# The second product of a mixture of experts in seven products for eight, on transposed sums

## The chip, the cores and the metric

The kernel runs on one core of a Trainium2 chip. Its metric is the time of one execution on the device in microseconds (us), as the median of several runs; the profile is that of one execution more.

## The reference

Three stages follow one another. An attention with 4 batches of 8 heads, 576 positions and head width 64 (a block-causal mask, softmax) gives x with 2304 tokens of 512 values. Then a mixture of 8 experts:

```python
def _moe_ref(x, w_gate, w1, w2):          # N, D, E, F = 2304, 512, 8, 1024
    logits = x @ w_gate
    P = np.exp(logits - logits.max())
    for _ in range(8):                    # rows, then columns, brought to their sums
        P /= P.sum(1, keepdims=True) + 1e-09
        P /= P.sum(0, keepdims=True) + 1e-09
        P *= N / E
    out = np.zeros((N, D), dtype=np.float32)
    for e in range(E):
        h = np.maximum(x @ w1[e], 0.0)
        out += P[:, e:e + 1] * (h @ w2[e])
    return out
```

Last comes a two-layer block with w_in (512 x 1024), a softmax-weighted activation, a normalisation and w_out (1024 x 512). Everything is float32, and a plain float32 product isn't what the kernel uses: it splits each operand into a high part that TensorE's fp32r format holds and a low rest, and makes three products of them (high x low, low x high, high x high).

## The kernel before, in words

All 2304 tokens are computed on one core. Attention comes first, and while it runs the first expert (expert 0) is filled in between, segment by segment of finished tokens: `moe` (L507) makes the hidden values of 128 columns of w1 at a time and then, tile by tile of 128 tokens, the second product, which it adds up in `accs` (L71, 18 tiles of 128 tokens x 512). `sinkhorn` (L390) brings the gate weights `pr` to their sums.

Experts 1 to 7 follow in three passes of 768 tokens (`work`, L810). A unit is half an expert's 1024 hidden columns, so there are 14 units in a pass and 42 in all. In a unit, `first_layer` (L642) computes a block of hidden values, transposed (hidden columns on the partitions, tokens along), with seven block products where eight would be plain: the 512 input values and the 768 tokens are cut into two halves each, and the unit's 512 hidden columns into two halves of two groups of 128 columns. The left factors (sums and differences of w1's blocks, numbered 1 to 7) are made and split by `left_factors` (L584) in pass 0, kept in DRAM (`fdram`, L86) and loaded again in passes 1 and 2; the right factors (of x) are made once per pass by `spread_x` (L551). The products run in the order "1627543", each for two groups of 128 columns, each group six matmuls of 384 columns (L653 to L655), into six PSUM banks of `l1p` that carry the running sums a, b and c. VectorE (DVE) adds between them (`plus`, L657), ScalarE (ACT) copies the first product out (r1, L677) before product 2 may add to its bank, and `hidden` (L662) makes the relu and its split on ACT and DVE. `second_layer` (L692) is a plain product: for each of six tiles of 128 tokens, twelve matmuls of 512 columns with the hidden values as the stationary operand and w2 as the moving one (L701 to L703), in the two banks of `mm`; DVE then adds the result, times the token's gate weight, to `accs` (L707).

In 32 of the 42 units one piece of w_in or w_out is decoded from float64 (`decode`, L439), mainly by DVE. `split_weights` (L428) puts a high part on ACT and the rest on GpSimd (POOL). All transfers are issued from SyncE's queue (SP), in order. The last stage (from L829) has per tile of 128 tokens four transposes (`early`, L841), 24 products of 512 columns in `front`, 16 short transposes, and 24 products in `back`.

The order of each engine's instructions isn't that of the text: it is fixed when the kernel is built by a planner that goes by the order of the text as priority and by what it expects to be ready, so one unit's first layer is interleaved with the second layer of the one before. What one engine waits for holds up all that stands behind it in its queue.

Of the kernel before, what the change touches and what calls it, by code (L numbers as in the profile page):

```python
# [18 lines left out]
P = 128  # L19
# [5 lines left out]
def build(ctx, tc, qT, kT, v, w_gate, w1, w1s, w2, w_in, w_out, g_ln, out):  # L25
# [12 lines left out]
    stg = xctx.enter_context(tc.tile_pool(name="stg", bufs=2, side="left"))  # L38
    dram = ctx.enter_context(tc.tile_pool(name="dram", bufs=1, space=bass.MemoryType.DRAM))
# [31 lines left out]
    accs = accp.tile([P, NT, DM], F32, name="acc")  # L71

    def acc(t):
        return accs[:, t, :]
# [11 lines left out]
    fdram = dram.tile([14, 11, P, 2, 512], F32, name="fd")  # L86
# [303 lines left out]
    def sinkhorn():  # L390
# [16 lines left out]
        for _ in range(8):  # L407
# [17 lines left out]
            yield  # L425

# [12 lines left out]
    def decode(i, half, src, scale=None):  # L439


        pair = wca.tile([P, 2, 512], F32R, tag="wa", name="w64")
# [64 lines left out]
    def moe(u, x, t0, w, tile0, mode=None):  # L507
# [21 lines left out]
        for j in range(w // P):  # L529
            t = tile0 + j  # L530
            ps = ytile()
            for c in range(4):
                hh = hs[c][:, 0, j * P : j * P + P]
                hl = hs[c][:, 1, j * P : j * P + P]
                nc.tensor.matmul(ps, hl, wz[c][:, 0, :], start=c == 0, stop=False)
                nc.tensor.matmul(ps, hh, wz[c][:, 1, :], start=False, stop=False)
                nc.tensor.matmul(ps, hh, wz[c][:, 0, :], start=False, stop=c == 3)
                if c < 3:
                    yield 3
            a = acc(t)  # L540
            if mode == "first":
                nc.scalar.copy(a, ps)
            else:
                nc.vector.tensor_tensor(a, ps, a, op=ALU.add)
            yield 3
# [3 lines left out]
    PRODUCTS = "1627543"  # L549

# [33 lines left out]
    def left_factors(u, p, stg):  # L584

        e, g = divmod(u, 2)
        pools = {i: (wca, "wa") for i in PRODUCTS}
        if u % 2:
            pools.update({i: (wcb, "wb") for i in PRODUCTS[:4]})
        W = {}  # L590

        def take(i):
            pool, tag = pools[i]
            W[i] = pool.tile([P, 2, 512], F32R, tag=tag, name=f"W{tag}")
            return W[i], fdram[u - 2, int(i) - 1]

        def split(i, a):
            t, kept = take(i)
            split_weights(t, a)
            nc.sync.dma_start(kept, r32(t))  # L600

        if p:
            for i in PRODUCTS:
                t, kept = take(i)
                nc.sync.dma_start(r32(t), kept)
        else:
            raw = {}
            for i, k in ((1, 1), (2, 1), (2, 2), (1, 2)):
                raw[i, k] = stg.tile([P, 512], F32, tag="raw", name="raw")
                nc.sync.dma_start(raw[i, k], w1s[e - 1, g, i - 1, k - 1])  # L610
            a11, a12, a21, a22 = raw[1, 1], raw[1, 2], raw[2, 1], raw[2, 2]
            s1 = stg.tile([P, 512], F32, tag="s1", name="s1", bufs=1)
            split("1", a11)
            nc.vector.tensor_tensor(s1, a21, a22, op=ALU.add)
            nc.vector.tensor_tensor(a21, a11, a21, op=ALU.subtract)
            nc.vector.tensor_tensor(a11, s1, a11, op=ALU.subtract)
            split("6", a11)
            split("2", a12)
            split("7", a21)
            split("5", s1)  # L620
            split("4", a22)
            nc.vector.tensor_tensor(a12, a12, a11, op=ALU.subtract)
            split("3", a12)
        return {i: t.rearrange("p s (k f) -> p s k f", k=2) for i, t in W.items()}

# [155 lines left out]
    for i in range(9):  # L781
# [3 lines left out]
        if i == 3:  # L785
            W = left_factors(2, 0, stg2)
# [185 lines left out]
```

## Time and profile before

| | |
|---|---|
| median of 3 runs | 2007.22 us (2005.99 to 2008.91) |
| profiled execution | 2010.55 us, its span 2008.8 us |
| instructions | 28989, of them 10101 matmuls |
| moved by DMA | 366.31 MB, 182 GB/s over the span |

The span is the time from the first to the last instruction of the profiled execution; 1.75 us of its time lie around it. Engines are PE (TensorE's matmuls), PEld (its weight loads, which run beside the matmuls), DVE, ACT, POOL and SP. A matmul's busy time includes its way through the array, and the next one starts before it has ended; so the time that a product costs is read from the distance between starts. L12 is line 12 of the kernel above.

### The profile page before, as it was taken

Reading aid. Unit: us, or ns where it says so; the run is one execution under the profiler, and the core shown is the slowest. Engines: PE = TensorE matmul, PEld = TensorE weight load, DVE = VectorE, ACT = ScalarE, POOL = GpSimd, SP = SyncE. Lnnn points to the kernel's source line nnn. Section 1 sums busy time; section 2 is a strip of 40 time slices with the busy share of each in tenths; the row PEclk is TensorE's granted clock in tenths of the full one; section 3 lists DMA queues with packets and bytes.
Section 4 is the critical chain, followed back from the end, with each engine's and each line's share of the span. In section 5 each row is a group of like instructions: output and inputs, shape, how many; then the busy total and the mean of one; then the engine's idle time right before and its main releaser. Section 6 shows DMA issues by size and latency. Waiting matters only on the chain.

```text
span 2008.8 us, 28989 instructions
## 1 busy us (share of the span) xinstructions
PE 1944.5 (97%) x10101; PEld 1724.0 (86%) x10101; DVE 1229.0 (61%) x2804; ACT 659.7 (33%) x1493; POOL 542.3 (27%) x582
## 2 busy tenths in 40 slices
PE   4798999889999999999999999999999999999999
PEld 4687998779999989889998998989989999988887
DVE  5867666575666667675454554565555455458774
ACT  5766656433333333331111111221112111124332
POOL 7765555276544445430000000010000000001000
PEclk8999999899999999999999999999999999999999
DMA  8665555145666577676555464665656556340000
GB/s 226 175 168 132 141 134 138 53 169 199 264 254 254 223 283 290 239 287 245 181 210 207 177 244 171 218 224 180 230 177 219 207 178 226 104 169 21 23 22 32
DMA packets 136944, 366.31 MB, mean 182 GB/s; under 512 B 17504, under 2 KB 29792, under 8 KB 136800
## 3 DMA queue, kind: packets, MB, share of 16 engines
q1 hardware_dynamic: 136800, 364.46, 53.0%
q8 instruction: 81, 1.33, 0.3%
q14 instruction: 63, 0.52, 0.1%
HBM read 237.52 MB, written 98.57 MB: 167 GB/s over the span
## 4 chain that ended last, share of the span: by engine, by line
PE 90%; DMA 4%; DVE 2%; issue 1%; POOL 1%; SPq 1%; ACT 1%; DVEq 0%; POOLq 0%; ACTq 0%
PE yps L701 12%; PE yps L703 11%; PE yps L702 11%; PE psb L653 4%; PE psb L654 4%; PE psb L655 4%; PE psa L653 3%; PE psa L655 3%; PE psa L654 3%; PE psc L655 3%; PE psc L653 3%; PE psc L654 3%; PE ops L908 2%; PE av L282 2%; PE ops L910 2%; PE ops L909 2%
## 5 line engine op out<-in xcount | busy, mean ns | idle before, releaser
L701 PE MATMUL yps<-w,h 128*128 128x512 f32 x1008 | 394.7, 393 | 0.2 <-DVE acc L707 0.2
L702 PE MATMUL yps<-w,h 128*128 128x512 f32 x1008 | 394.2, 391 | 0.0
L703 PE MATMUL yps<-w,h 128*128 128x512 f32 x1008 | 391.9, 391 | 0.0
L707 DVE SCALAR_TENSOR_TENSOR acc<-yps,pr,acc 128x512 f32<-128x512 f32 x252 | 186.3, 748 | 319.6 <-PE yps L703 319.5
L430 POOL TENSOR_TENSOR w<-f,w 128x256 fp32r<-128x256 f32 x32 | 23.6, 738 | 771.9 <-ACT w L429 733.6
L703 PEld LDWEIGHTS yps<-w,h 128*128 128x128 f32 x1008 | 189.3, 188 | 41.2
L701 PEld LDWEIGHTS yps<-w,h 128*128 128x128 f32 x1008 | 189.2, 188 | 33.2 <-DVE acc L707 0.8
L702 PEld LDWEIGHTS yps<-w,h 128*128 128x128 f32 x1008 | 189.3, 188 | 31.4
L664 ACT ACTIVATE h<-vu 128x384 fp32r<-128x384 f32 x168 | 87.6, 525 | 309.1 <-DVE vu L659 309.0
L430 POOL TENSOR_TENSOR w<-raw,w 128x512 fp32r<-128x512 f32 x96 | 132.6, 1388 | 56.6 <-ACT w L429 56.1
L659 DVE TENSOR_TENSOR u<-psb,r 128x384 f32<-128x384 f32 x168 | 92.4, 553 | 52.0 <-PE psb L655 48.7
L665 DVE SCALAR_TENSOR_TENSOR h<-vu,h 128x384 fp32r<-128x384 f32 x168 | 114.1, 682 | 12.9 <-ACT h L664 10.6
L659 DVE TENSOR_TENSOR vu<-psc,u 128x384 f32<-128x384 f32 x168 | 92.3, 553 | 38.1 <-PE psc L655 37.5
L653 PE MATMUL psb<-X,Wwa 128*128 128x384 f32 x336 | 113.0, 336 | 0.0
L655 PE MATMUL psb<-X,Wwa 128*128 128x384 f32 x336 | 112.9, 336 | 0.0
L654 PE MATMUL psb<-X,Wwa 128*128 128x384 f32 x336 | 112.9, 336 | 0.0
L655 PE MATMUL psc<-X,Wwa 128*128 128x384 f32 x336 | 112.6, 335 | 0.0
L653 PE MATMUL psc<-X,Wwa 128*128 128x384 f32 x336 | 112.6, 335 | 0.0
L654 PE MATMUL psc<-X,Wwa 128*128 128x384 f32 x336 | 112.5, 335 | 0.0
L664 ACT ACTIVATE h<-psa 128x384 fp32r<-128x384 f32 x84 | 41.0, 491 | 217.2 <-PE psa L655 213.6
L224 POOL TENSOR_SCALAR e<-e,sv 128x128 f32<-128x128 f32 (+2 forms) x144 | 81.6, 570 | 100.8 <-DVE sv L220 44.6
L430 POOL TENSOR_TENSOR Wwa<-raw,Wwa 128x512 fp32r<-128x512 f32 x56 | 81.0, 1453 | 74.9 <-ACT Wwa L429 74.9
(201 smaller groups left out, 4492.6 us busy)
## 6 DMA issues: line engine op xcount, KB each, us to landing
Wwa<-fd SPq DMA_DIRECT2D x140, 512.0 KB, 4.3
w<-fd SPq DMA_DIRECT2D x112, 512.0 KB, 5.9
fd<-Wwa SPq DMA_DIRECT2D x70, 512.0 KB, 3.9
fd<-w SPq DMA_DIRECT2D x56, 512.0 KB, 5.2
Wwb<-fd SPq DMA_DIRECT2D x56, 512.0 KB, 3.8
raw<-in_w SPq DMA_DIRECT2D x96, 256.0 KB, 4.1
raw<-in_w1s SPq DMA_DIRECT2D x56, 256.0 KB, 4.9
fd<-Wwb SPq DMA_DIRECT2D x28, 512.0 KB, 3.7
```

The source lines that it names most:

```text
L224: nc.gpsimd.tensor_scalar(e, e, self.rs, 1.0, op0=ALU.mult, op1=ALU.mult)
L430: nc.gpsimd.tensor_tensor(t[:, 1, :], raw, r32(t[:, 0, :]), op=ALU.subtract)
L653: nc.tensor.matmul(ps, wh, xl, start=start and kc == 0, stop=False, skip_group_check=True)
L654: nc.tensor.matmul(ps, wh, xh, start=False, stop=False, skip_group_check=True)
L655: nc.tensor.matmul(ps, wl, xh, start=False, stop=stop and kc == 1, skip_group_check=True)
L659: nc.vector.tensor_tensor(t, bank[g, a], tmp[g, "r1" if a == "b" else name[1:]], op=ALU.add)
L664: nc.scalar.activation(h[:, 0], src, AF.Relu)
L665: nc.vector.scalar_tensor_tensor(h[:, 1], src, 0.0, r32(h[:, 0]), op0=ALU.max, op1=ALU.subtract)
L701: nc.tensor.matmul(ps, hl, ws[c][:, 0, :], start=c == 0, stop=False)
L702: nc.tensor.matmul(ps, hh, ws[c][:, 1, :], start=False, stop=False)
L703: nc.tensor.matmul(ps, hh, ws[c][:, 0, :], start=False, stop=c == 3)
L707: nc.vector.scalar_tensor_tensor(a, ps, pr[:, t, e : e + 1], a, op0=ALU.mult, op1=ALU.add)
```

## The change

In pass 0 (tokens 0 to 767) experts 1 to 7 are computed as before. In passes 1 and 2 the second product is made of seven block products too. Its hidden values are multiplied by the token's gate weight before they are used (relu and weight in one DVE operation), w2's factors are the stationary operand and the hidden values' factors the moving one, so that the output comes transposed (output columns on the partitions, tokens along) and each of the seven products can be summed over all 14 units by itself. The seven sums of 768 values per partition lie where `accs` was and in a new tile; they are combined once, at the end of a pass, by `finish_pass`, which also adds expert 0's share and stores the result in DRAM (`rdram`). The factors of w2 are made in pass 0 by `second_weights` and kept beside those of w1. The factors of the hidden values are made in each unit from the four blocks by three POOL subtractions and one on DVE, and split by ACT and POOL. The seven products of a unit come after the first layer of the next unit. Weights are held in one pool of 11 buffers where there were 7, 4 and 6. Expert 0's second product is transposed for tokens from 768 on and kept in DRAM until `finish_pass`; pass 0's sums wait in DRAM as well (`adram`), and the last stage loads both, the second kind without transposes.

The diff, cut to its core (what is left out are allocations, moved lines and the unchanged parts of the functions):

```diff
 def moe(u, x, t0, w, tile0, mode=None):
...
+        if tile0 < 6:
...
+            return
+        for j in range(4):
             ps = ytile()
             for c in range(4):
+                hh, hl = (hs[c][:, s, 0:w] for s in range(2))
+                wh, wl = (wz[c][:, s, j * P : j * P + P] for s in range(2))
+                nc.tensor.matmul(ps[:, 0:w], wh, hl, start=c == 0, stop=False)
+                nc.tensor.matmul(ps[:, 0:w], wl, hh, start=False, stop=False)
+                nc.tensor.matmul(ps[:, 0:w], wh, hh, start=False, stop=c == 3)
...
+SECOND = "3175624"
+def load_factors(u, layer):
+    W = {}
+    for i in PRODUCTS if layer == 0 else SECOND:
+        t = weight_tile()
+        nc.sync.dma_start(r32(t), fdram[u - 2, 7 * layer + int(i) - 1])
+        W[i] = by_halves(t)
+    return W
 def second_weights(u):
...
+        def keep(f, a):
+            t = weight_tile()
+            tk = by_halves(t)
+            nc.scalar.copy(tk[:, 0], a)
+            nc.gpsimd.tensor_tensor(tk[:, 1], a, r32(tk[:, 0]), op=ALU.subtract)
+            nc.sync.dma_start(fdram[u - 2, 6 + f], r32(t))
+        nc.vector.tensor_tensor(s1, a21, a22, op=ALU.add)
+        keep(5, s1)
...
+def weighted_hidden(R, Pb):
+    B = {}
+    def hidden(g, i, j, src):
+        if g == 0:
+            B[i, j] = hb.tile([P, 2, BLK], F32, tag="hb", name="hb")
+        nc.vector.scalar_tensor_tensor(
+            B[i, j][:, g, :], src, 0.0, Pb[:, (j - 1) * BLK : j * BLK], op0=ALU.max, op1=ALU.mult
+        )
+    def split(f, a):
+        R[f] = hf.tile([P, 2, 2, BLK], F32R, tag="hf", name="hf")
+        hi, lo = R[f][:, 0], R[f][:, 1]
+        nc.scalar.copy(hi, a)
+        nc.gpsimd.tensor_tensor(lo, a, r32(hi), op=ALU.subtract)
+    def minus(o, a, b, eng=nc.gpsimd):
+        eng.tensor_tensor(o, a, b, op=ALU.subtract)
+        return o
+    def steps():
+        b22, b11, b12, b21 = B[1, 1], B[2, 2], B[2, 1], B[1, 2]
+        split("3", b22)
+        yield
+        split("1", b11)
+        yield
+        split("7", minus(hb.tile([P, 2, BLK], F32, tag="hb", name="hb"), b22, b12))
+        yield
+        split("5", minus(b12, b12, b11))
+        yield
+        split("6", minus(b11, b22, b12))
+        yield
+        split("2", b21)
+        yield
+        split("4", minus(b21, b21, b11, nc.vector))
+        yield
+    return hidden, steps()
+def second_products(V, R, first):
+    n = 0
+    for f in SECOND:
+        for g in range(2):
+            pool, tag = (mm, "mm") if n % 4 == 3 else (l1p, "l1")
+            n += 1
+            ps = pool.tile([P, 512], F32, tag=tag, name="yps")[:, 0:BLK]
+            product(V[f], R[f], ps, g, True, True)
+            a = summed(f, g)
+            if first:
+                nc.scalar.copy(a, ps)
+            else:
+                nc.vector.tensor_tensor(a, ps, a, op=ALU.add)
+        yield
+def gate_weights(e, p):
+    t = pbp.tile([P, 2 * BLK], F32, tag="pb", name="pb")
+    nc.sync.dma_start(
+        t.rearrange("p (t q) -> p t q", q=P), pdram[6 * p : 6 * p + 6, e, :].partition_broadcast(P)
+    )
+    return t
+def finish_pass(p):
...
+    add(g, "2", "1")
+    add(v, "6", "1")
+    add(v, "7", "6")
+    add(g, "6", "5")
+    add(v, "4", "7")
+    add(v, "7", "5")
+    add(g, "3", "6")
+    Pb = gate_weights(0, p)
+    for f, i, j in (("4", 1, 1), ("7", 1, 0), ("2", 0, 1), ("3", 0, 0)):
+        y = hb.tile([P, 2, BLK], F32, tag="hb", name="y0")
+        n0 = (2 * (p - 1) + j) * BLK
+        nc.sync.dma_start(y, ydram[:, 2 * i : 2 * i + 2, n0 : n0 + BLK])
+        w = Pb[:, None, j * BLK : (j + 1) * BLK].to_broadcast([P, 2, BLK])
+        g.tensor_tensor(y, y, w, op=ALU.mult)
+        s = summed(f).rearrange("p (k n) -> p k n", k=2)
+        v.tensor_tensor(s, s, y, op=ALU.add)
+        nc.sync.dma_start(rdram[:, 2 * i : 2 * i + 2, n0 : n0 + BLK], s)
...
+work = [(p, u) for p in (1, 2) for u in range(2, 16)]
+before = None
+for n, (p, u) in enumerate([*work, (3, 2)]):
+    if n < len(work):
+        if u % 2 == 0:
+            Pb = gate_weights(u // 2, p)
+        R = {}
+        hidden, steps = weighted_hidden(R, Pb)
+        first_layer(W, X, hidden)
+        late_decode(n + 14)
+    if before:
+        for _ in second_products(*before):
+            next(steps, None)
+    run(steps)
+    if n < len(work):
+        if n + 1 < len(work):
+            if work[n + 1][0] > p:
+                X = {}
+                run(spread_x(p + 1, X))
+            W = load_factors(work[n + 1][1], 0)
+        before = load_factors(u, 1), R, u == 2
+    if u == 2 and p > 1:
+        finish_pass(p - 1)
...
 def early(t):
...
+        if t < 6:
+            if t > 1:
+                nc.sync.dma_start(x, adram[:, t * DM : t * DM + DM])
+            src = mm.tile([P, 4, P], F32, tag="mm", name="xtp")
             for c in range(4):
+                nc.tensor.transpose(src[:, c, :], x[:, c * P : c * P + P], ident)
+        else:
+            src = x.rearrange("p (c q) -> p c q", c=4)
+            nc.sync.dma_start(src, rdram[:, :, (t - 6) * P : (t - 5) * P])
```

## Rows read from the trace of the kernel before

**Rows 1.** The page, parts 1 and 2: busy time of the engines; PE in 40 slices.
```profile
PE 1944.5 (97%) x10101; PEld 1724.0 (86%) x10101; DVE 1229.0 (61%) x2804; ACT 659.7 (33%) x1493; POOL 542.3 (27%) x582
...
PE   4798999889999999999999999999999999999999
```

**Rows 2.** Windows of passes 0 to 2, last stage: PE, PEld, DVE, ACT, POOL; PEclk, DMA, GB/s.
```profile
467.00:904.00 437.00, 437.00 (x2191) 395.56 (x2190) 294.55 (x439) 157.56 (x308) 219.22 (x160) 1.00 0.71 264
904.00:1342.00 438.00, 438.00 (x2192) 396.11 (x2191) 235.06 (x459) 83.08 (x170) 19.22 (x22) 1.00 0.58 205
1342.00:1779.00 437.00, 436.84 (x2177) 393.77 (x2176) 223.72 (x433) 74.08 (x150) 9.57 (x13) 1.00 0.55 195
1779.00:2008.80 229.80, 225.59 (x1228) 183.38 (x1226) 163.67 (x452) 79.84 (x126) 18.82 (x18) 1.00 0.11 40
```

**Rows 3.** The page, part 4: the chain that ended last, by engine and line.
```profile
PE 90%; DMA 4%; DVE 2%; issue 1%; POOL 1%; SPq 1%; ACT 1%; DVEq 0%; POOLq 0%; ACTq 0%
PE yps L701 12%; PE yps L703 11%; PE yps L702 11%; PE psb L653 4%; PE psb L654 4%; PE psb L655 4%; PE psa L653 3%; PE psa L655 3%; PE psa L654 3%; PE psc L655 3%; PE psc L653 3%; PE psc L654 3%; PE ops L908 2%; PE av L282 2%; PE ops L910 2%; PE ops L909 2%
```

**Rows 4.** Timeline of PE: 48 first-layer products; then 24 second-layer ones (start, us).
```profile
470.29 0.34 PE L653 MATMUL psb<-X,Wwa 128*128 128x384 f32 x1
...
478.64 0.39 PE L701 MATMUL yps<-w,h 128*128 128x512 f32 x1
...
1306.16 0.39 PE L701 MATMUL yps<-w,h 128*128 128x512 f32 x1
...
1311.62 0.34 PE L655 MATMUL psa<-X,Wwb 128*128 128x384 f32 x1
```

**Rows 5.** Groups by form: busy us, mean ns of one, idle before it and releaser.
```profile
L707 DVE SCALAR_TENSOR_TENSOR acc<-yps,pr,acc 128x512 f32<-128x512 f32 x252 | 186.3, 748 | 319.6 <-PE yps L703 319.5
L659 DVE TENSOR_TENSOR u<-psb,r 128x384 f32<-128x384 f32 x168 | 92.4, 553 | 52.0 <-PE psb L655 48.7 <-ACT r L677 2.1
L665 DVE SCALAR_TENSOR_TENSOR h<-psa,h 128x384 fp32r<-128x384 f32 x84 | 46.5, 555 | 41.2 <-ACT h L664 40.7
L677 ACT COPY r<-psa 128x384 f32<-128x384 f32 x84 | 39.2, 477 | 93.7 <-PE psa L655 93.6
```

**Rows 6.** Lines 665, 430 and 622: shortest, median and longest ns of one.
```profile
L665 DVE SCALAR_TENSOR_TENSOR h<-vu,h x168: 541/550/1652, 480.0 to 1765.2; 128x384 fp32r<-128x384 f32 x168
...
L430 POOL TENSOR_TENSOR w<-raw,w x96: 1256/1297/1788, 9.2 to 883.8; 128x512 fp32r<-128x512 f32 x96
...
L430 POOL TENSOR_TENSOR w<-f,w x32: 731/738/744, 741.1 to 1714.8; 128x256 fp32r<-128x256 f32 x32
...
L622 DVE TENSOR_TENSOR raw<-raw x14: 1730/1768/1778, 411.5 to 853.1; 128x512 f32<-128x512 f32 x14
```

**Rows 7.** Timeline of DVE and POOL at the change of pass, alone and together.
```profile
1332.24 1.02 POOL L572 TENSOR_TENSOR t<-b,b 128x384 f32<-128x384 f32 x1 [17.48 <-DVE acc L707]
...
1333.16 0.55 DVE L560 TENSOR_TENSOR X<-b,X 128x384 fp32r<-128x384 f32 x1
...
1333.34 1.24 POOL L573 TENSOR_TENSOR b<-b,b 128x384 f32<-128x384 f32 x1
...
1333.84 1.15 DVE L560 TENSOR_TENSOR X<-t,X 128x384 fp32r<-128x384 f32 x1
```

**Rows 8.** DMA issues (KB each, us to landing); the window with most traffic.
```profile
w<-fd SPq DMA_DIRECT2D x112, 512.0 KB, 5.9
...
520.00:560.00 40.00, 40.00 (x203) 36.31 (x202) 21.74 (x33) 12.88 (x25) 21.26 (x16) 1.00 0.84 326
```

**Rows 9.** Timeline of PE in the last stage: eight transposes between two products.
```profile
1792.81 0.39 PE L857 MATMUL h<-w,x 128*128 128x512 f32 x1
1793.04 1.04 PE L844 MATMUL xtp<-ident,acc 128*128 128x128 f32 x8
1793.83 0.49 PE L855 MATMUL h<-w,x 128*128 128x512 f32 x1
```

**Rows 10.** Window on the ramp of the last stage; columns as in rows 2.
```profile
1800.00:1820.00 20.00, 20.00 (x115) 16.32 (x114) 19.22 (x62) 8.51 (x13) 2.09 (x2) 1.00 0.00 1
```

More of the change, by code (lines that the diff above doesn't have):

```diff
@@ L602, in left_factors @@
[L602 to L623, printed above, removed]
@@ new lines, in second_weights, with product @@
+        nc.vector.tensor_tensor(a11, s1, a11, op=ALU.subtract)
+        keep(6, a11)
+        nc.vector.tensor_tensor(a12, a12, a11, op=ALU.subtract)
+        keep(3, a12)
+        return ws
+    def product(w, x, ps, g, start, stop):
+        for kc in range(2):
+            wh, wl = (w[:, s, kc, g * P : g * P + P] for s in range(2))
+            xh, xl = (x[:, s, kc, :] for s in range(2))
+            nc.tensor.matmul(ps, wh, xl, start=start and kc == 0, stop=False, skip_group_check=True)
+            nc.tensor.matmul(ps, wh, xh, start=False, stop=False, skip_group_check=True)
+            nc.tensor.matmul(ps, wl, xh, start=False, stop=stop and kc == 1, skip_group_check=True)
@@ L645, in first_layer @@
+    def first_layer(W, X, hidden):
         bank = {}
         tmp = {}
-        def product(i, ps, g, start, stop):
-            w, x = W[i], X[i]
-            for kc in range(2):
-                wh, wl = (w[:, s, kc, g * P : g * P + P] for s in range(2))
-                xh, xl = (x[:, s, kc, :] for s in range(2))
-                nc.tensor.matmul(ps, wh, xl, start=start and kc == 0, stop=False, skip_group_check=True)
-                nc.tensor.matmul(ps, wh, xh, start=False, stop=False, skip_group_check=True)
-                nc.tensor.matmul(ps, wl, xh, start=False, stop=stop and kc == 1, skip_group_check=True)
@@ new lines, in summed @@
+    def summed(f, g=None):
+        i = 2 * (int(f) - 1)
+        t, o = (accs, i) if i < 8 else (accs2, i - 8)
+        if g is None:
+            return t[:, o * BLK : (o + 2) * BLK]
+        return t[:, (o + g) * BLK : (o + g + 1) * BLK]
+    def second_products(V, R, first):
[8 more added lines that the diff above has]
+                if first:
+                    nc.scalar.copy(a, ps)
+                else:
+                    nc.vector.tensor_tensor(a, ps, a, op=ALU.add)
+            yield
@@ L780, in build @@
     W = None
-    for i in range(9):
+    for i in range(10):
         next(rounds)
@@ L826, in build @@
         if 8 <= n < 40:
             decode(*late[n - 8])
-        second_layer(u, p, ws, hs)
+    ws = second_weights(2)
+    for u in range(2, 16):
+        hs = {}
+        first_layer(W, X, plain_hidden(hs))
+        if u < 15:
+            W, nws = first_factors(u + 1, stg), second_weights(u + 1)
+        else:
+            X = {}
+            run(spread_x(1, X))
+            W = load_factors(2, 0)
+        late_decode(u - 2)
+        second_layer(u, 0, ws, hs)
+        ws = nws
+    nc.sync.dma_start(adram, accs)
@@ new lines, in build @@
+    rctx.close()
+    wip = ctx.enter_context(tc.tile_pool(name="wip", bufs=8, side="right"))
+    xin = ctx.enter_context(tc.tile_pool(name="xin", bufs=2, side="right"))
+    w2p = ctx.enter_context(tc.tile_pool(name="w2p", bufs=8, side="right"))
+    wi = [[load_decoded(wip, 2 * dc + f) for f in range(2)] for dc in range(4)]
+    early0 = [xin.tile([P, DM], F32, tag="x", name="xin") for t in range(2)]
+    for t in range(2):
+        nc.sync.dma_start(early0[t], adram[:, t * DM : t * DM + DM])
```

191 lines of the change are left out of this document (114 added, 77 removed).

## The prediction

> **What bounds the kernel now.** I read the page first: TensorE (PE) is busy in 1944.5 of 2008.8 us, and its row of the 40 slices is at 9 from the tenth slice on [rows 1]. The windows by stage say where: between 467 and 1779 us, the three passes of experts 1 to 7, PE is busy for 1311.8 of 1312 us, at a granted clock of 1.00, its upper level of 2.4 GHz [rows 2]. The chain of waits agrees: 90% of it is PE, a third the three lines of the second product [rows 3]. So in this stage a shorter list of matmuls is shorter time, as long as nothing else takes PE's place. In pass 1 the others have room: VectorE (DVE) 235.06 of 438 us, ScalarE (ACT) 83.08, GpSimd (POOL) 19.22, DMA 0.58 [rows 2].
>
> **The matmuls.** The stage has 42 units (3 passes, 14 half experts) in 1312 us, 31.24 us each. A unit is 84 products of 384 columns (first layer) and 72 of 512 (second). In the timeline 48 products of 384 columns take 478.64 - 470.29 = 8.35 us, 0.1740 each, and 24 of 512 take 1311.62 - 1306.16 = 5.46 us, 0.2275 each [rows 4]. By these a unit is 14.61 + 16.38 = 30.99 us; the other 0.25 us are seams where the two kinds meet. In 28 of the 42 units the change replaces the 72 by 84 of exactly the first layer's form (same weights' shape, 384 columns). That saves 16.38 - 14.61 = 1.77 us, or, if the seams go too, 31.24 - 29.22 = 2.02. I take 1.85: 28 x 1.85 = **51.8 us** (49.6 to 56.6).
>
> The saving rests on products costing their columns. Rows: from 384 to 512 columns the step grows by 0.0535 us, 0.418 ns a column, which leaves only 13 ns that a product costs by itself [rows 4]. The Trainium skill, "TensorE: Matmul & The Clock Gate", section on the back-to-back issue gap, has a sustained 81 ns for 128 and 131 ns for 512 columns, so mostly a fixed price per product; by that (an estimate: 114 ns at 384) 84 products would take as long as the 72, and the change would save nothing here.
>
> **The last stage.** Twelve of 18 tiles come back from DRAM already transposed, so 12 x 4 transposes go. Eight of them lie between two products that stand 1.02 us apart instead of 0.2275 [rows 9], so 0.099 each: 48 x 0.099 = **4.8 us**, all on PE's path. Six tiles come by a load of the same size instead of from SBUF; two of these loads are started ahead, the others at least a tile's time (12 us) ahead.
>
> **What the units of passes 1 and 2 add beside PE**, per unit of some 29.3 us:
> - DVE: 6 accumulations of 512 (0.748) go, 14 of 384 (0.553, the price of the same operation in the first layer) and one subtraction of 768 (twice 0.550) come; the eight operations on the hidden values stay eight [rows 5, 6]. 235.06 / 14 = 16.8 us now, so 16.8 - 4.5 + 7.7 + 1.1 = 21.1 us, 72%.
> - POOL: now one 256-wide operation per decode (0.738). Seven splits and three subtractions of 768 come. 512 wide takes at least 1.256, 256 wide 0.738 [rows 6], so 768 some 1.78: 17.8 + 0.7 = 18.5 us, 63%.
> - ACT: eight relus go, seven copies of 768 come; at 0.48 for 384 [rows 5] this is about even.
> - DVE and POOL together: with both inputs in SBUF a DVE operation beside a POOL one took 1.15 instead of 0.55 us, and POOL's 1.24 instead of 1.02 [rows 7]; with one input in PSUM DVE's stay at 0.555 on the mean [rows 5]. The accumulations read PSUM. Two-SBUF operations are 11 per unit: two of the hidden values (the block whose sum lies in SBUF), the subtraction, eight of a decode. At 0.6 us x POOL's 63% that is 4.4 us more for DVE: 25.5 of 29.3. POOL goes to 21. Both still fit.
> - DMA and SP: 14 loads of 512 KB instead of 11, 251 GB/s, and a decode's 18, where now 205 run. Between 520 and 560 us 326 GB/s moved with PE busy for 40.00 of 40 us [rows 8]. A load lands in 5.9 us [rows 8]; with 11 buffers it is asked for ten pairs of products (21 us) ahead. SP waits for the buffer's release with the later loads, decoded weights and gate rows queued behind it. The ten pairs hide that; if the cover went, each late load would cost its 5.9 us.
>
> Second products run one unit behind, so each split operand has a whole unit (29 us) for a POOL chain of 21 us, paced by the eight hf buffers. I cost the units' stalls at 0.1 us each, 3 us (0 to 27, the second rival).
>
> **Once-only places.** Pass 0 keeps its products, and gets four more splits per unit on POOL (219.22 / 14 = 15.7 to 20.9 us) and four more DVE operations, 1.77 at worst beside POOL [rows 6], so DVE 294.55 / 14 = 21.0 to at most 28.1 of 31.24; its writes grow by 1.5 MB, to 314 GB/s. It fits: 2 us (0 to 10). Expert 0's second product for the late tiles has the same columns in narrower products, and the gate weights two transposes: 1 us (0 to 3). Pass 0 to 1: two first layers in a row, nothing to fill in, fresh buffers over old ones: 2 (0 to 5). Pass 1 to 2: seven POOL operations of 1.78, 12.5 us, and seven DVE additions empty the sums, and ACT may write the first new sum only after the last old one is stored. There are 14.6 us of first layer and eight banks of 1.04 us for it, but POOL also has its splits: 3 (0 to 15). Last unit: its splits have 14.6 us of cover instead of 29, though its products take them one by one every 2.1 us: 2 (0 to 6). Then eight DVE additions of 768 (1.1 alone, 2.2 beside POOL) fall on the ramp of the last stage, where DVE is busy for 19.22 of 20 us [rows 10]: 4 (0 to 17).
>
> **The sum.** 51.8 + 4.8 = 56.6 saved, 3 + 2 + 1 + 2 + 3 + 2 + 4 = 17 given back: 39.6 net. The profiled execution took 2010.55 us, so 1971; it stands 3.3 above the median of 2007.22, so **1968** for the median.
>
> **Rivals.**
> 1. *Slower: DVE blocked by POOL.* Place: the 11 two-SBUF operations of a unit, with POOL 63% busy in passes where it now has 4%. Each wait delays the accumulations queued behind it, and so the PSUM banks PE waits for. DVE has 31.24 - 21.1 = 10.1 us until a unit is no shorter than now: 0.92 us per operation decides. Rows: 0.6 beside POOL, but the longest hidden operation is 1.652 against 0.550, 1.10 more [rows 6], and POOL's operations get longer than any now. At 1.0 us DVE needs 32.1 per unit, 28 x 0.9 = 25 us more than now, with 4.8 saved and 14 lost elsewhere 2041; at 1.10, 2072. Against it: over a third of the operations would find POOL idle, and pass 0 has POOL at 50% with no idle PE. Chance 0.14. The Trainium skill, "SBUF — State Buffer", section on who interferes with whom, states this as a rule: a DVE instruction with two SBUF inputs and a GpSimd instruction that reads SBUF lock each other out for the whole instruction. The trace agrees: the DVE operation of [rows 7] ends 0.41 us after POOL's.
> 2. *Part of it lost: ACT behind POOL.* ACT's copies for the splits wait for POOL's three subtractions, and the r1 copy that PE needs before factor 2 stands in the same queue. It has the 2.09 us of factor 6; behind one subtraction, a copy and itself it takes 1.78 + 0.8 + 0.48 = 3.06. If so in each unit, 28 x 0.97 = 27 us: 1995. For it: ACT's queue has never had to wait for POOL in this stage; against: the same copies have a unit of slack, and can stand behind r1. Chance 0.16, everything from 1988 to 2003 counted.
> 3. *No gain:* the product count, not the columns, sets the time; then 4.8 are saved and 17 lost, 2007.2 + 12 = 2019, or 2002 if nothing is lost. The 0.418 ns a column speak against it: 0.03.
>
> **How the numbers follow.** The forecast, 1950 to 1988 (all of the saving and no loss gives 1950.6; the sum with the larger bounds of the tail and the pass change 1990): 0.67. The range 1950 to 1997 takes in most of rival 2 and leaves out rivals 1 and 3. A measurement of this kernel tells 0.2% (4 us) from no change. Faster by more: forecast and rival 2, 0.82. Same: 0.04. Slower: 0.14.
>
> **What would show it.** Right: units of 29.2 to 29.5 us between 904 and some 1725 us, PE without gaps, 0.174 us steps in the second product, DVE about 25 and POOL about 21 us per unit, twelve tiles without transposes. Wrong: the accumulations late behind two-SBUF operations of 1.5 us and more with PE waiting for them (rival 1); r1 late and PE idle before factor 2 (rival 2); 0.19 us steps or more (rival 3); PE waiting on loads (DMA); idle PE of over 10 us at the change of pass 1 to 2 or at the start of the last stage (these terms mis-sized).

## The result: 24 us faster, and the profile after

The changed kernel takes 1982.98 us (median of 4 runs, 1979.82 to 1983.93), the kernel before, in the same session, 2006.61. The ratio is 0.9879, with a 95% interval of 0.9862 to 0.9896. That is 1.2% faster, clear of the noise, and inside the range given (1950 to 1997), but 15 us above the forecast of 1968: of the 39.6 us forecast some 24 came. The profiled execution took 1983.74 us, with a span of 1982.0; against that of before the gain is 26.8.

The page first: busy time, PE and its granted clock in 40 slices, the chain (compare [rows 1, 3]).

```profile
PE 1898.4 (96%) x10487; PEld 1762.7 (89%) x10487; DVE 1454.0 (73%) x3104; ACT 743.3 (38%) x1555; POOL 1163.6 (59%) x920
...
PE   5899999889999999999999999998999999989999
...
PEclk8999999999999999999999999998999999989999
...
PE 77%; DVE 9%; DMA 4%; POOL 4%; issue 3%; ACT 1%; SPq 1%; DVEq 0%; POOLq 0%; ACTq 0%
```

PE is still the bound, but its share of the chain fell from 90% to 77%, and DVE took 9%. PE and clock both dip in the same two slices, around 1362 and 1760 us. The windows say the same: two inside passes 1 and 2, the change of pass between them, the ramp of the last stage (columns as in [rows 2]).

```profile
1000.00:1280.00 280.00, 280.00 (x1605) 280.00 (x1604) 194.41 (x377) 70.04 (x101) 182.53 (x107) 1.00 0.80 278
1290.00:1390.00 100.00, 86.67 (x449) 82.94 (x448) 83.44 (x113) 26.02 (x47) 76.03 (x42) 0.93 0.72 253
1390.00:1730.00 340.00, 339.77 (x1943) 338.92 (x1942) 241.82 (x466) 80.80 (x116) 224.76 (x130) 1.00 0.80 280
1730.00:1785.00 55.00, 46.60 (x237) 40.06 (x236) 41.66 (x86) 11.90 (x20) 21.60 (x12) 0.91 0.58 216
```

Inside the passes next to nothing is lost: 280 us for 1605 products is 0.1745 us each, 29.3 for a unit of 168. In the 100 us around the change of pass PE is idle for 13.3 us, and the clock is lower besides.

Groups that answer to [rows 5, 6, 8], and the loads of factors:

```profile
L770 POOL TENSOR_TENSOR hf<-hb,hf 128x768 fp32r<-128x768 f32 x196 | 368.4, 1895 | 94.9 <-ACT hf L769 94.9
...
L773 POOL TENSOR_TENSOR hb<-hb 128x768 f32<-128x768 f32 x84 | 158.8, 1891 | 161.6 <-DVE hb L762 160.1
L816 DVE TENSOR_TENSOR acc<-yps,acc 128x384 f32<-128x384 f32 x364 | 192.6, 549 | 67.6 <-PE yps L710 66.9
...
W<-fd SPq DMA_DIRECT2D x392, 512.0 KB, 5.6
```

The new operations cost about what was taken for them: 0.549 us for an accumulation (0.553), 1.89 for 768 columns on POOL (1.78, so 6% more), and a load lands in 5.6 us.

**Where the time went.** For each matmul I took the distance to the next start less the median distance of its form (174 ns for 384 columns, 229 for 512, and so on): what is left is lost time, idle PE and lower clock together. Summed from all of PE's timeline, in us:

| stretch of the span | lost before | lost after | difference | the prediction's term |
|---|---|---|---|---|
| to 467 (attention, expert 0) | 84.3 | 64.5 | -19.8 | +1 |
| 467 to 860 (pass 0) | 1.6 | 11.5 | +9.9 | +2 |
| 860 to 1000 (pass 0 to 1) | 0.4 | 5.9 | +5.5 | +2 |
| 1000 to 1280, 1390 to 1730 (units) | 2.1 | 3.4 | +1.3 | +3 |
| 1280 to 1390 (pass 1 to 2) | 0.4 | 22.2 | +21.8 | +3 |
| 1730 to 1785 (last unit, ramp) | 1.2 | 12.2 | +11.0 | +2 and +4 |
| from 1785 | 2.8 | 2.5 | -0.3 | 0 |

The products by their nominal distances fell from 1898.5 to 1843.5 us: 55.0 saved, forecast 56.6, less 1 for expert 0's. Given back: 29.4, forecast 17. So the saving was right, and what was given back is far from where it was looked for: a gain of 20 at the start that no step had, and losses of 48 in four places that had 13.

**The change of pass.** The waits of PE there (line waited for, total us, times, longest), and DVE in the middle of it:

```profile
PE yps L708 <- DVE hb L762: 8.0, 3, 4.3
```

```profile
1353.88 2.19 DVE L762 SCALAR_TENSOR_TENSOR hb<-vu,pb 128x384 f32<-128x384 f32 x1
...
1359.59 1.90 DVE L474 TENSOR_SCALAR b<-w 128x256 uint32<-128x256 uint32 x1
...
1362.29 0.54 DVE L762 SCALAR_TENSOR_TENSOR hb<-psc,pb 128x384 f32<-128x384 f32 x1
1362.76 1.81 DVE L468 SCALAR_TENSOR_TENSOR a<-w,a 128x256 uint32<-128x256 uint32 x1
1364.49 0.55 DVE L720 TENSOR_TENSOR psc<-psc,u 128x384 f32<-128x384 f32 x1
1364.96 2.10 DVE L850 TENSOR_TENSOR acc<-acc,y 128x768 f32<-128x768 f32 x1
1366.98 2.02 DVE L471 SCALAR_TENSOR_TENSOR a<-w,a 128x256 uint32<-128x256 uint32 x1
1368.93 0.54 DVE L762 SCALAR_TENSOR_TENSOR hb<-psc,pb 128x384 f32<-128x384 f32 x1
```

Between 1362.8 and 1368.9 DVE has to give free a PSUM bank (L762 on psc) that PE's next product wants. Ahead of it stand two decode operations of 1.8 and 2.0 us and an addition of `finish_pass` (L850), and PE waits 4.25 us for it. The same decode operations inside pass 1, and POOL at the same moment:

```profile
L468 DVE SCALAR_TENSOR_TENSOR a<-w,a 128x256 uint32<-128x256 uint32 x9 | 3.8, 417 | 0.0
L474 DVE TENSOR_SCALAR b<-w 128x256 uint32<-128x256 uint32 x9 | 2.6, 285 | 0.0
```

```profile
1362.44 1.84 POOL L773 TENSOR_TENSOR hb<-hb 128x768 f32<-128x768 f32 x1 [1.09 <-DVE hb L773]
1364.24 6.44 POOL L770 TENSOR_TENSOR hf<-hb,hf 128x768 fp32r<-128x768 f32 x3
```

0.417 us on the mean in the unit, 1.81 here: the DVE operations that have their inputs in SBUF and meet one of POOL's end 0.15 to 0.8 us after POOL's does (L468 at 1364.57, L773 on POOL at 1364.28; then three of POOL's to 1370.68, 2.1 us each). Those that read PSUM (L762 on psc, L720) still take 0.54. The Trainium skill, "SBUF — State Buffer", section on who interferes with whom, calls the port the two share an exclusive lock, held for a whole instruction; the 1.8 to 2.1 us agree, beside POOL's 1.84. L474 has one SBUF input and waits too (1.90 against 0.285).

PE's timeline there shows a second cost, the clock:

```profile
1354.91 0.34 PE L710 MATMUL yps<-hf,W 128*128 128x384 f32 x1
1357.52 0.44 PE L708 MATMUL yps<-hf,W 128*128 128x384 f32 x1 [2.27 <-DVE hb L762]
...
1358.31 0.52 PE L708 MATMUL yps<-hf,W 128*128 128x384 f32 x1
1358.63 0.52 PE L709 MATMUL yps<-hf,W 128*128 128x384 f32 x1
...
1360.87 0.52 PE L710 MATMUL yps<-hf,W 128*128 128x384 f32 x1
1362.89 0.44 PE L708 MATMUL yps<-hf,W 128*128 128x384 f32 x1 [1.49 <-DVE hb L762]
...
1369.53 0.69 PE L708 MATMUL yps<-hf,W 128*128 128x384 f32 x1 [4.25 <-DVE hb L762]
```

After the 2.27 us of idle time the products from 1357.99 us on stand 0.32 us apart instead of 0.175: the granted clock from 1358.0 to 1361.4 us is 0.50, the lower of its two levels, 1.2 GHz. Eight of them from 1358.31 to 1360.87 cost 1.2 us more. Before, no such stretch lay between 423 us and the end of the span's last products; after, there were six from 470 us to 1775, each behind a stall.

### The profile page after: what moved, and what is told of

It reads as the page before. It is cut to its first block, busy times and chain, and to the rows that moved or that the text cites. A ratio compares the mean times of both kernels' runs of the same rounds, so it can differ in the third digit from the quotient of the medians.

```text
span 1982.0 us, 31143 instructions
## 1 busy us (share of the span) xinstructions
PE 1898.4 (96%) x10487; PEld 1762.7 (89%) x10487; DVE 1454.0 (73%) x3104; ACT 743.3 (38%) x1555; POOL 1163.6 (59%) x920
## 4 chain that ended last, share of the span: by engine, by line
PE 77%; DVE 9%; DMA 4%; POOL 4%; issue 3%; ACT 1%; SPq 1%; DVEq 0%; POOLq 0%; ACTq 0%
PE yps L708 5%; PE yps L710 5%; PE yps L709 5%; PE psb L709 4%; PE psb L708 4%; PE psb L710 4%; PE yps L862 3%; PE yps L864 3%; PE yps L863 3%; PE psc L710 2%; PE psc L708 2%; PE psc L709 2%; PE psa L708 2%; PE psa L710 2%; PE psa L709 2%
## 5 line engine op out<-in xcount | busy, mean ns | idle before, releaser
L770 POOL TENSOR_TENSOR hf<-hb,hf 128x768 fp32r<-128x768 f32 x196 | 368.4, 1895 | 94.9 <-ACT hf L769 94.9
L769 ACT CAST hf<-hb 128x768 fp32r<-128x768 f32 x196 | 160.5, 836 | 490.4 <-POOL hb L773 158.5
L708 PE MATMUL yps<-hf,W 128*128 128x384 f32 x784 | 268.1, 342 | 10.5 <-DVE hb L762 8.2
L709 PE MATMUL yps<-hf,W 128*128 128x384 f32 x784 | 267.1, 341 | 0.0
L710 PE MATMUL yps<-hf,W 128*128 128x384 f32 x784 | 263.8, 341 | 0.0
L773 POOL TENSOR_TENSOR hb<-hb 128x768 f32<-128x768 f32 x84 | 158.8, 1891 | 161.6 <-DVE hb L762 160.1
L816 DVE TENSOR_TENSOR acc<-yps,acc 128x384 f32<-128x384 f32 x364 | 192.6, 549 | 67.6 <-PE yps L710 66.9
L708 PE MATMUL psb<-X,W 128*128 128x384 f32 x504 | 169.7, 337 | 1.4 <-ACT acc L814 1.4
L709 PE MATMUL psb<-X,W 128*128 128x384 f32 x504 | 169.3, 336 | 0.0
L710 PE MATMUL psb<-X,W 128*128 128x384 f32 x504 | 167.7, 335 | 0.0
L708 PEld LDWEIGHTS yps<-hf,W 128*128 128x128 f32 x784 | 149.0, 190 | 13.1 <-DVE hb L762 9.8
L709 PEld LDWEIGHTS yps<-hf,W 128*128 128x128 f32 x784 | 149.1, 190 | 0.0
L720 DVE TENSOR_TENSOR u<-psb,r 128x384 f32<-128x384 f32 x168 | 91.1, 550 | 79.1 <-PE psb L710 71.4
L710 PEld LDWEIGHTS yps<-hf,W 128*128 128x128 f32 x784 | 148.7, 190 | 0.0
L862 PE MATMUL yps<-w,h 128*128 128x512 f32 x336 | 133.3, 397 | 5.5 <-DVE acc L868 2.7
L446 POOL TENSOR_TENSOR W<-raw,W 128x512 fp32r<-128x512 f32 x84 | 117.7, 1416 | 29.7 <-ACT W L445 29.7
L864 PE MATMUL yps<-w,h 128*128 128x512 f32 x336 | 132.6, 395 | 0.0
L863 PE MATMUL yps<-w,h 128*128 128x512 f32 x336 | 132.5, 394 | 0.0
L1102 POOL TENSOR_SCALAR lh<-ln 128x1024 f16<-128x1024 f32 x18 | 19.1, 1059 | 187.4 <-DVE ln L1099 65.2
L708 PE MATMUL psa<-X,W 128*128 128x384 f32 x336 | 113.5, 338 | 2.9 <-ACT W L445 1.5
```

The source lines that it names most:

```text
L446: nc.gpsimd.tensor_tensor(t[:, 1, :], raw, r32(t[:, 0, :]), op=ALU.subtract)
L708: nc.tensor.matmul(ps, wh, xl, start=start and kc == 0, stop=False, skip_group_check=True)
L709: nc.tensor.matmul(ps, wh, xh, start=False, stop=False, skip_group_check=True)
L710: nc.tensor.matmul(ps, wl, xh, start=False, stop=stop and kc == 1, skip_group_check=True)
L720: nc.vector.tensor_tensor(to, bank[g, a], tmp[g, "r1" if a == "b" else name[1:]], op=ALU.add)
L769: nc.scalar.copy(hi, a)
```

## The experiments

Ratios are against the kernel before, which ran beside each.

**The change of pass without the arithmetic of `finish_pass`.** Its additions, products and the loads for them are left out, so the output is another; the stores stay.

```diff
-        add(g, "2", "1")
...
-            g.tensor_tensor(y, y, w, op=ALU.mult)
-            v.tensor_tensor(s, s, y, op=ALU.add)
```

> The changed kernel without the arithmetic of finish_pass: the seven additions of sums, expert 0's share and its gate weights are left out, the four stores stay. Theory: at the change of pass 1 to 2 VectorE's operations with two inputs in SBUF and GpSimd's take turns, each waiting for the other's end, and the 15 operations of finish_pass are what makes both late; then most of the 22 us that TensorE loses between 1290 and 1390 us goes, 12 to 18 us, and of the 14 us at the ramp of the last stage few, since loads are late there: 1983 - 17 = 1966, between 1960 and 1970. Rival: the new X factors, the decode and the splits are late there by themselves; then at most 5 us go, 1978 or more.

A single run gave 1962.95 us, 20 less than the changed kernel. Lost from 1280 to 1390: 12.5 us (22.2); on the ramp 7.2 (12.2); in pass 0 7.1 (11.5), which this edit doesn't touch. So the arithmetic of `finish_pass` makes some 10 us at the change, under the 12 to 18 expected, and 5 on the ramp; 12 us at the change remain without it. (Four kernels that leave the change of pass as it is lost 19.3 to 22.9 us there, so differences of 7 and more tell.)

**No decode around the change of pass.**

```diff
-            late_decode(n + 14)
+            if n not in (14, 15):
+                late_decode(n + 14 if n < 14 else n + 12)
```

> The changed kernel with no decode in the first two units of pass 2; each later decode moves two units back, the last two into units that had none. The eight VectorE operations of the decode took 11.2 us there instead of 2.8 alone. Theory (locked out by GpSimd): without them VectorE is 10 us ahead and the stall at the change of pass falls by 8 to 14 us, to 1969 to 1975. Rival (plain load): only their own 2.8 us count, 1980 or a little under.

1978.14 us, ratio 0.9860 (0.9843 to 0.9877). Lost at the change: 14.5 us in place of 22.2. The decode's part is 8 us, just short of the theory's 8 to 14; the ramp took 4 of it back (15.9 us lost), perhaps because the last two decodes went into late units that had none, which no run tried apart. So the total came near the rival's 1980, and not for the rival's reason.

**Expert 0's share added inside the pass**, three of its four parts at the 6th, 8th and 10th unit:

```diff
+        if n < len(work) and u in (7, 9, 11):
+            share(p, gate_weights(0, p), *{7: ("4", 1, 1), 9: ("2", 0, 1), 11: ("3", 0, 0)}[u])
```

> The changed kernel with three of expert 0's four shares added in the middle of a pass (units 7, 9 and 11), where VectorE and GpSimd have room, instead of at its end. The same work, six of finish_pass's 15 operations earlier. Theory (turns between VectorE and GpSimd at the change of pass): the stall there falls from 22 us by 6 to 12, and the ramp's a little: 1970 to 1976, with no new idle time in units 7 to 12. Rival: the chain of the seven sums itself (each addition waiting for the one before and the store for the last) is what counts; then 0 to 4 us, 1979 to 1983.

1989.13 us, ratio 0.9911: slower than the change by 6. At the change of pass it did what was expected (15.3 us lost), but inside the passes 14.7 us were lost in place of 3.4. DVE was not full there, but idle:

```profile
1631.91 0.29 DVE L465 TENSOR_SCALAR a<-w 128x256 uint32<-128x256 uint32 x1 [5.42 <-DMA w<-in_w_out]
```

```profile
1634.52 0.45 PE L708 MATMUL yps<-hf,W 128*128 128x384 f32 x1 [3.11 <-DVE hb L762]
```

L465, a decode's first operation, waits for the decode's load, and the operation that frees PE's bank stands behind it. Each of the seven stalls inside the passes that cost over 0.4 us follows such a wait of 2.6 to 5.4 us, 9 of the 14.7 us in all; the operations behind it take their short times (0.29 and 0.42 us), so POOL isn't what holds them up. Between 1390 and 1730 us DVE waits 21.3 us for these loads, where the changed kernel waits 12.7. Why they come later (the loads that go with the moved additions, or their order) was not tried.

**Six of pass 0's decodes moved into passes 1 and 2**, as second decodes of six units:

```diff
-        late_decode(u - 2)
...
+            if n in (3, 5, 7, 9, 18, 20):
+                decode(*late[(3, 5, 7, 9, 18, 20).index(n)])
```

> The changed kernel with the six decodes of pass 0 moved into units of passes 1 and 2 (a second decode in units 5, 7, 9 and 11 of pass 1 and 6 and 8 of pass 2). TensorE lost 11.5 us in pass 0 before 860 us and 6 more up to 1000, in the units with a decode. Theory: a decode's eight VectorE operations, each behind one of GpSimd's, are what doesn't fit beside the new factors; then pass 0 loses 2 to 4 us instead, and the doubled units show a few us of new idle time: 1972 to 1979. Rival: the new factors alone overfill VectorE; then pass 0 still loses over 8 us, and the time is 1983 or more.

1999.07 us (10 runs), ratio 0.9967 (0.9951 to 0.9983): 16 us worse than the change. Pass 0 lost 6.0 us in place of 11.5; but two kernels that leave pass 0 as it is lost 5.7 and 7.1 there, so that says little. From 860 to 1280 and 1390 to 1730 the loss rose from 9.3 to 27.3. The total lies in the rival's range, the loss in pass 0 doesn't. In the units with two decodes the second one meets POOL: from 1116.55 to 1127 us its operations take 1.4 to 1.9 us each and stand between the accumulations whose banks PE waits for:

```profile
PE psa L708 <- DVE acc L816: 2.6, 4, 1.3
```

**The ramp: all six loads of the sums ahead.**

```diff
-    xin = ctx.enter_context(tc.tile_pool(name="xin", bufs=2, side="right"))
+    xin = ctx.enter_context(tc.tile_pool(name="xin", bufs=6, side="right"))
...
-    for t in range(2):
+    for t in range(6):
```

> The changed kernel with six buffers instead of two for the last stage's first tiles, and all six loads of pass 0's sums asked for ahead of w_out's. Theory: on the ramp of the last stage TensorE waits for these loads, queued on SP behind w_out's eight and the four stores, 5.6 us by its own waits, and runs at the lower granted clock from 1764 to 1774 us for it; with the loads ahead 8 to 12 us go: 1971 to 1975. Rival: VectorE's additions of finish_pass hold the ramp up anyway; then under 4 us go: 1979 or more.

1981.33 us, ratio 0.9882: no change clear of noise, and 12.9 us lost on the ramp. The wait for the loads was gone, and PE waited 8.6 us for the softmax (L1072 there) instead. What that waits for is seen in the changed kernel's timeline of DVE:

```profile
1764.03 1.33 DVE L1057 TENSOR_TENSOR x<-xtp,x 128x512 fp32r<-128x512 f32 x2 [6.06 <-ACT x L1056]
1766.32 0.06 DVE L1039 MEMSET magic<- 128x1 uint32 x1 [0.96 <-DMA rd<-acc]
1766.33 2.36 DVE L1069 TENSOR_REDUCE nm<-h 128x1 f32<-128x1024 f32 x2
```

L1039 writes a constant of the last stage; it waits for a store (`rd<-acc`, of the last sums), since its small tile lies where those sums lie. The softmax's first step (L1069) stands behind it. The rival's number came, but not its reason: what holds the ramp is this store and not the additions.

**The same tiles over other memory:** the pool of w_out on the other side, so that the small tiles behind it no longer lie over the sums.

```diff
-    wop = ctx.enter_context(tc.tile_pool(name="wop", bufs=8, side="left"))
+    wop = ctx.enter_context(tc.tile_pool(name="wop", bufs=8, side="right"))
```

> The changed kernel with w_out's eight tiles on the other side of SBUF, so that the last stage's small tiles no longer lie where the seven sums lay. With the loads ahead alone the ramp didn't get shorter: VectorE's first operation of the last stage (the constant, and the maximum behind it) waited for the store of those sums until 1760.3 us, and TensorE waited 8.9 us for the bank that this maximum holds. Theory: this reuse of memory is what holds the ramp; without it VectorE's maximum comes right after the products and 6 to 10 us of TensorE's 12 to 16 lost us go, 1973 to 1977, if the loads of the first tiles don't take its place. Rival: those loads (two buffers) are the limit as soon as this one is gone; then under 3 us go, 1980 or more.

1971.67 us (1969.23 to 1975.17), ratio 0.9824 (0.9809 to 0.9838): 11 us less than the change by one word. The same constant now comes at its place, and the ramp loses 4.8 us. PE waits for no load of the sums there either, though these have two buffers as in the changed kernel:

```profile
1749.59 0.06 DVE L1039 MEMSET magic<- 128x1 uint32 x1
...
1759.10 1.21 DVE L1069 TENSOR_REDUCE nm<-h 128x1 f32<-128x1024 f32 x1
```

**Both repairs, and then `finish_pass` on DVE alone.**

```diff
-        v, g = nc.vector, nc.gpsimd
+        v, g = nc.vector, nc.vector
```

> Both repairs together: the last stage's small tiles lie over other memory than the sums of passes 1 and 2, and no decode falls into the two units around the change from pass 1 to pass 2. Theory: the two losses lie in different places (1740 to 1780 us, and 1290 to 1390 us) and add up. The first alone gave 1971.7, the second alone took 4.8 us off; so 1964 to 1969, with 14 to 16 us of lost TensorE time at the change and under 6 on the ramp of the last stage. Rival: the tail takes back what the change gives, since the run of the second alone had a tail of 15.8 in place of 12 us; then 1970 to 1973.

> The kernel of both repairs, and the seven operations of finish_pass that GpSimd had (three additions, four products with the gate weight) go to VectorE, so that finish_pass gives VectorE 15 operations and GpSimd none. Theory (the turns of the two engines set the loss at the change): VectorE's operations of 768 take 0.95 to 1.2 us each instead of 2.0 to 2.6, 15 of them 14 to 18 us, no more than the eight took with their turns; TensorE's loss at the change falls to 8 to 12 us, the total by 2 to 6. Rival (VectorE's plain amount of work sets it, with the splits of the same units still beside it on GpSimd): seven more operations on VectorE hold the sums and the hidden values up for longer, the loss at the change grows to 18 us or more and the total by 2 to 8.

Both repairs: 1969.56 us (4 runs), ratio 0.9810 (0.9797 to 0.9824), the fastest of the kernels that compute everything, but not to be told from the one repair of the tiles: the change of pass lost 15.8 us in place of 22.2, as the theory had it, and the ramp 9.3 in place of 4.8, as the rival had it. The total lies half a microsecond under the rival's range. With `finish_pass` on DVE: 1973.03 us, ratio 0.9826 (0.9813 to 0.9840), and 16.6 us lost at the change. Neither side's loss came: `finish_pass` gave DVE fifteen operations of 1.0 to 1.6 us on the mean, 22.0 us in all, where the eight of 1.3 to 2.3 us took 16.2. They are shorter, but there are more of them. The total's 3.5 us more fit the rival's 2 to 8, but lie ahead of the edit: the attention ended at 376.2 us instead of 371.8, and up to 860 us 5 us more were lost.

**The start.** Three edits of the kernel before. First its token blocks in the order that the change gives them; then also expert 0's second product transposed as in the change (its output, left so, is in another order).

```diff
-        blocks = ((0, 512),) if seg == 0 else ((0, 384), (384, 256))
+        blocks = ((0, 512),) if seg == 0 else ((0, 256), (256, 384))
```

> The kernel before with one thing of the change alone: expert 0's second segment in blocks of 256 and 384 tokens instead of 384 and 256. The attention of the changed kernel ended at 372.1 us of its span, that of the kernel before at 386.3, though neither edit touches attention. Theory: the order of the blocks alters the planner's filling of attention, so attention ends 14 us earlier here too and the median is near 1990 us. Rival 1: the transposed second product of expert 0 does it; then attention ends near 386 us here and the median stays at 2007. Rival 2: the difference is that of one execution to another; then attention ends near 386 or 372 without order and the time stays at 2007.

```diff
+        if tile0 >= 6:
...
+                    nc.tensor.matmul(ps[:, 0:w], wh, hl, start=c == 0, stop=False)
...
+                if mode == "first":
+                    nc.scalar.copy(y, ps[:, 0:w])
+                else:
+                    nc.vector.tensor_tensor(y, ps[:, 0:w], y, op=ALU.add)
```

> The kernel before with the blocks of 256 and 384 tokens and, from token 768 on, expert 0's second product on transposed sums as in the changed kernel; the sums lie turned where the plain ones lay, so the later stages add to them in the wrong order and the output isn't the reference's. With the blocks alone attention ended at 384.3 us and 2000.7 was the median. Theory: the transposed product (narrower pieces, so the planner can put them into smaller holes) is what lets attention end at 372 in the changed kernel; then it ends within 4 us of 372 here and the median falls by 10 to 15 us below 2000.7, to 1986 to 1991. Rival: something else in the changed kernel's first stage (the tiles of its other pools, the second transfer of the gate weights); then attention stays at 382 to 386 and the median near 2000.

Blocks: 2000.69 us, ratio 0.9974 (0.9961 to 0.9987), the attention's last product at 384.3 us (before 386.3, after the change 372.1). With the transposed product: 1999.5, ratio 0.9960 (0.9945 to 0.9975), 379.3 us. So the two edits bring 7 of the attention's 14 us; of what was expected only the time of the second's rival came. The rows of the attention in the kernel before show a stall, first on ACT, then on PE:

```profile
176.61 0.68 ACT L130 ACTIVATE qhigh<-qraw 128x576 fp32r<-128x576 f32 x1 [3.19 <-issue]
```

```profile
171.68 0.33 SPq L122 DMA_DIRECT2D qraw<-in_qT  x1
```

```profile
PE tp L229 <- DVE a L253: 3.0, 1, 3.0
```

ACT's copy of q stands in its queue where q, asked for at 171.68 us, has not landed; DVE waits for the copy and PE for DVE. In the changed kernel the same load is issued at 168.40 us, where the whole attention is some 2 us ahead already; ACT waits 0.54 us for it, and PE 0.8 us. With the two edits above, PE's wait there was still 2.9 us. The edit gives q two tiles in turn, so that its load needn't wait until the last q has been spread:

```diff
-    kraw, qraw = (sp.tile([P, S], F32, name=f"{i}raw") for i in "kq")
+    kraw, *qraws = (sp.tile([P, S], F32, name=f"{i}raw") for i in ("k", "q", "r"))
...
+        qraw = qraws[n // 2 % 2]
```

> The kernel before with one thing changed, in the attention: the raw q of a pair of heads is loaded into two tiles in turn, so that its load needn't wait until the one before has been spread. In the kernel before, the load that was issued at 171.7 us came too late for the copy of q's high part, which held ScalarE's queue for 3.2 us and, behind it, VectorE for 2.5 and TensorE for 3.0 us at 178, with a stretch of the lower clock after it; in the changed kernel the same load was issued 3.3 us earlier and the stall isn't there. Theory (that stall is a good part of the 14 us that the attention gained, and has nothing to do with the change's products): the stall and the lower clock after it go, the attention ends at 376 to 381 us in place of 386, the total at 1997 to 2002. Rival (the stall only moves: other copies of q or other operations hold the queues elsewhere): the attention ends at 384 to 387 us and the total stays at 2004 to 2008.

> The changed kernel with both repairs (other memory for the last stage's small tiles; no decode around the change from pass 1 to pass 2), and q's raw load in two tiles in turn. Theory: this kernel's attention has already lost the stall, so only what is left of waits for q goes: 0 to 3 us, 1966 to 1970. Rival: in the attention there is as much to gain here as in the kernel before, 5 us or more, 1961 to 1965.

Kernel before with it: 2001.91 us (10 runs), ratio 0.9976 (0.9967 to 0.9986), a gain of 5 us. The attention ended at 374.0 us, 12.3 earlier, without the lower clock at 180 us. The same q, in the second tile now, is asked for a pair of heads earlier, and ACT's copy at 168.01 us doesn't wait for it:

```profile
146.89 0.45 SPq L123 DMA_DIRECT2D rraw<-in_qT  x1
```

```profile
PE tp L230 <- POOL e L225: 1.4, 2, 1.0
```

That is the theory, and the end is earlier still than it said; but to 467 us the loss fell by 8.2 only (84.3 to 76.1), so part was given back between the attention and pass 0. The edit also takes away more than the one stall: ACT's idle time ahead of its sixteen copies of q falls from 28.7 to 5.9 us. The changed kernel with both repairs and this: 1972.18 us, ratio 0.9822 (0.9803 to 0.9842). No gain; both numbers were too low, and the stall was indeed gone there already.

## Why the prediction was right, and where it was not

The bound, the saving and the direction were foreseen. That the time fell into the range given is luck in part: without the 20 us gained at the start, which no step had, it would stand near 2003 us, above the range's 1997.

- **The matmuls** (51.8 us): right. In the second product 34 steps take 1181.00 - 1175.02 = 5.98 us, 0.176 each, against 0.229 of the 512 wide:

```profile
1175.02 0.34 PE L709 MATMUL yps<-hf,W 128*128 128x384 f32 x1
...
1181.00 0.34 PE L710 MATMUL yps<-hf,W 128*128 128x384 f32 x1
```

  In these rows columns set the time, and the third rival (a price per product) is out. The Trainium skill's figure beside it ("TensorE: Matmul & The Clock Gate", section on the back-to-back issue gap, 131 ns for 512 columns) differs from the 229 ns measured, and the measurement decides. A unit takes 29.3 to 29.4 us, as forecast.
- **The last stage** (4.8 us): right. 24 transposes of the sums remain of 72; at this form's median distance of 0.109 us that is 5 us.
- **The units' stalls** (3 us): 1.3. DVE has 194.41 / 280 x 29.3 = 20.3 us a unit where 25.5 were forecast, POOL 19.1 for 21. The step that failed is the price of 0.6 us for eleven two-SBUF operations. Four of the decode's eight (L465, L474, L479, L485) read one tile of SBUF only, and seven of the eight cost no more inside the units (0.285 to 0.417 us), because POOL stands idle then, waiting for the unit's hidden values (L773 waits 160 us for L762 in all); only the two on `vu` are late (1.041 us on the mean against 0.541 alone).
- **First rival** (DVE blocked by POOL, slower): out for the units, but its mechanism is the one that bites where POOL is never idle. It was priced once per unit, and the price was due at the places that occur once.
- **Pass 1 to 2** (3 us): the mis-sized term, 21.8. The prediction had POOL's seven operations and DVE's seven additions in it, and left out that a decode's operations and the unit's two on `vu` queue among them, most at 1.4 to 2.2 us in place of 0.3 to 0.55. Its own sign for this term came, over 10 us of idle PE there. The runs show some 10 us from `finish_pass` and 8 from the decode, each left out alone; both together were not. The splits of the next x (L599) lie at the same place and were not tried apart. That these together hit PSUM banks, and not sums, was not foreseen: the wait named was for ACT's first copies.
- **Pass 0** (2 us) and **pass 0 to 1** (2): 9.9 and 5.5. The step that failed is that DVE, at most 28.1 of 31.24 us a unit, fits. In busy time it fits (336.28 of 437 us from 467 to 904); but at 847 to 852 us three decode operations (L468, L471, L477) of 1.0 to 1.1 us instead of 0.41 stand ahead of the relu (L751) that PE waits 2.4 us for. That decode is the cause of the whole is argued from such rows, not shown: the loss in pass 0 was 5.7 to 12.7 us among kernels with the same pass 0.
- **The tail** (4) and **last unit** (2): 11 together, no PE stall in the last unit itself. The eight additions are there, 11 us of DVE between 1740 and 1785, and with them in place the ramp lost 4.8 us once the tiles lay elsewhere, so their price was about right. What the step lacked is the other 7 us, a wait that the prediction had not listed at all: a new tile over old sums.
- **Expert 0** (+1 us): -19.8, the largest miss, and on the other side. The attention's own code is unchanged, so the planner's order is what moved; a stall on q's load is gone that the edit of q's tile removes in the kernel before too. By the runs that edit and the blocks' order are worth 5 and 6 us. Whether they add up was not run, and the rest of the 20 stays open.
- **Second rival** (ACT behind POOL): out. PE waits for r1 (L733) 0.2 us between 780 and 960 us, and not in the units.

The profile's gain is 12.8 us short of the forecast: 1.6 less saved, 12.4 more given back, and 1.2 better ahead of the first and behind the last product. The direction, the bound and the mechanism of the saving were right; the sizes of the once-only places were not. One sum of the prediction is off, with nothing resting on it: with the larger bounds of the tail and the pass change it gives 1968 + 13 + 12 = 1993, not 1990.

## What to carry to other kernels

- Cost the places that occur once by the queue, not by busy shares: list what stands ahead of the operation that frees PE's bank, each at the price it has beside POOL, and each load that one of them waits for. Here four places took 48 us of 55 saved.
- Where a stage ends in stores, look at which later tiles lie over the stored memory: one pool moved to the other side gave 11 us.
- When the order is a planner's, a change in one place can move time in another, here 20 us at the start; find it in the profile before it is credited to the change.

## What was not expected of the hardware

- A stall of 2.3 us in the middle of a busy stage was followed by products at the lower clock (0.32 us for 384 columns instead of 0.175), so this stall cost more than its idle time; the next one, 1.49 us of idle time up to 1362.89, was followed by steps of 0.175.
- DVE's operations with one SBUF input (L465, 0.294 us, and L474, 0.285 us) waited for POOL just as those with two did (1.35 and 1.90 us).
